# Attention and a two-layer network on one core: four engines in the order of the text from the first instruction on, w_in's units between a pair's steps, w_out's behind the layer's tiles

## The chip, the cores and the metric

The kernel runs on one core of a Trainium2 chip. The metric is device microseconds for one execution of the whole kernel, as the median of several runs. The engines are TensorE (PE: matrix products, written to PSUM), VectorE (DVE), ScalarE (ACT: functions of one element, here also scaled copies), GpSimd (POOL: here a few operations on one column) and SyncE (SP), whose queue issues all DMA transfers. Each engine runs its own queue in order and waits on semaphores for the others.

## The reference

```python
def _attn_ref(q, k, v):                      # (8, 12, 448, 64) each, f32
    S = q.shape[2]
    scale = 1.0 / np.sqrt(q.shape[-1])
    scores = scale * np.matmul(q, k.transpose(0, 1, 3, 2)) - np.log(S)
    attn = 1.0 / (1.0 + np.exp(-scores))
    return np.matmul(attn, v).astype(np.float32)

def _moe_ref(x, w_in, w_out):                # (3584, 768), (768, 2048), (2048, 768)
    h = x @ w_in
    g = np.where(h > 0.0, h, 1.0 * (np.exp(np.minimum(h, 0.0)) - 1.0))
    return (g @ w_out).astype(np.float32)
```

The output of the attention, with the heads laid side by side for each token, is the x of the second function. The weights w_in and w_out are 64-bit floating point in memory.

## The kernel before

**The work.** There are 8 batches, and a batch has 6 pairs of heads. A pair takes these steps: `prepare` (maxima of its inputs, powers of two as scales, and the operands in the form in which PE takes them), then for four blocks of keys (three of 128 and a rest of 64, `NC` = 3 is the rest's number) `scores` (PE), `soften` (a sigmoid on ACT), `parts` (the weights split into two 16-bit parts, on ACT and DVE) and `values` (PE, all blocks into one PSUM tile, `pav`), and at the end `finish` (the result, split into two parts, goes to `xh`). When a batch has its six pairs, `hidden` first rescales `xh` (`rescale`) and then runs the first layer, `moe1`: 16 tiles of the hidden dimension (`NF` = 16), 18 matmuls each into a tile `ph`, then an exponential on ACT, two operations on DVE, and a split into `g`. The second layer, `moe2`, is a generator: each `next` gives one step of six matmuls into `po`. From batch 1 on, `fill(n)` puts n such steps of the batch before between the steps of a pair.

Batch 0 (`EXACT` = 1) computes scores and values in f32. From batch 1 on each operand is two f16 parts and a product is three matmuls; but the pairs below `WHOLE` = `EXACT * NP + 2` = 8, so the first two of batch 1, still use f32 values: for them `parts` does nothing and v is loaded a second time, as a whole tile.

**The weights.** Both arrive as 64-bit words and are turned into f32 and then into two scaled f16 parts, once. For w_in this is done for 16 tiles of 768 KB (`load_w_in`, `w_in_tile`), beside batch 0. A tile takes five operations of some 0.9 us each and a chain of small ones: in `magnitudes` two on ACT (`Abs` of the high word, and the top of the low word, lines 156 and 160), one on DVE (line 161), and matmuls against ones on PE that add up the magnitudes (line 168); `sum_magnitude` reduces these sums to a power of two, one column of `wp`; `signed` puts the sign back (DVE, line 175); `split` writes the two parts (ACT line 139, DVE line 140). The words wait in a tile with the tag "wo", in a ring of five buffers, `WR` = 5; the results, f32, stand in another five, `WT` = 5. When all of w_in is done, the tile `wo` takes the same memory.

For w_out it is the same in two halves of 384 columns (`load_w_out`, a generator): 16 tiles of `magnitudes` and `signed`, then one sum for the half (in the PSUM tag "pav", one buffer, which a pair's values use as well), then 16 splits. That makes 32 steps a half. The loads (384 KB each, line 247) go to the tag "at" (3 buffers) or to places in `wo` that are still unused, and SP waits at a load until its place is free. `step(n)` runs n steps.

**The order.** Tile objects carry the dependencies, and the framework sets the semaphores. Outside `tc.manual_schedule` the framework's scheduler chooses the order of the instructions on each engine by its own estimate of their durations. Inside, the four engines named there take their instructions in the order of the text:

```python
    with tc.manual_schedule(engines={E.PE, E.Activation, E.DVE, E.SP}):
        for b in range(EXACT, B):
```

So before, batch 0's attention, all of w_in, the first layer of batch 0 and most of w_out (58 of its 64 steps, asked for in `w_out_beside`, four a tile) are ordered by the scheduler; the pairs of batch 1 and all that follows are ordered by the text. The other six steps of w_out, if any are left by then, stand in the first three pairs of batch 1. POOL is ordered by the scheduler throughout.

Of the kernel before, what the change touches and what calls it, by code (L numbers as in the profile page):

```python
# [34 lines left out]
def attention_ffn(  # L35
# [114 lines left out]
    def magnitudes(t, lo, hi, hl, sums, start, stop):  # L150


        u, h = t.bitcast(U32), hi.bitcast(F32)


        nc.scalar.activation(t, h, AF.Abs, scale=2.0**-112)
# [3 lines left out]
        nc.scalar.activation(lo, top, AF.Copy, scale=2.0**-13, bias=2.0**-14 - 0.5)  # L160
        nc.vector.scalar_tensor_tensor(
            u, u, 3, lo, op0=ALU.logical_shift_left, op1=ALU.bitwise_or
        )

# [14 lines left out]
    def sum_magnitude(dst, sums):  # L179

        m = sb.tile([P, 1], F32, tag="alw", name="alw", bufs=2)
        nc.vector.tensor_reduce(m, sums, axis=AX.X, op=ALU.max)
        nc.vector.tensor_scalar(m, m, TINY, None, op0=ALU.max)
# [18 lines left out]
    def w_in_tile(f):  # L202
        lo, hi, hl = w_in_words[f]
        t = stage[0][:, WR * 2 + f % WT].rearrange("p (c x) -> p c x", c=NK)
        sums = ps.tile([P, 512], F32, tag="pm", name=f"si{f}", bufs=3)
        magnitudes(t, lo, hi, hl, sums[:, :P], True, True)
        sum_magnitude(wp[:, f : f + 1], sums[:, :P])
        nc.vector.reciprocal(wr[:, f : f + 1], wp[:, f : f + 1])
        s = sb.tile([P, 1], F32, tag="sw", name=f"swi{f}", bufs=2)
        nc.gpsimd.tensor_scalar(s, wr[:, f : f + 1], 2.0**WTOP, None, op0=ALU.mult)  # L210
        d = wi[:, :, :, f * P : (f + 1) * P]
        signed(t, hi)
        split(d[:, 0], d[:, 1], t, s)
# [6 lines left out]
    def load_w_out(wo):  # L220


        for i in range(NH):
# [6 lines left out]
            sums = ps.tile([P, 512], F32, tag="pav", name=f"so{i}")  # L230
            loads = []

            def load(f):
                if f >= NF:
                    return
                if i == 0 and f >= 2:
                    st = wo[:, 1, f % 8 * 2 :][:, :2]
                elif i == 1 and f % 2 and f < NF - SP - SKEW:
                    st = wo[:, 1, NF - SP + f // 2 % 2 * 2 :][:, :2]
                else:  # L240
                    st = None
                if st is None:

                    st = sb.tile([P, 1, HM], U64, tag="at", name=f"so{i}_{f}", bufs=AB)
# [5 lines left out]
                loads.append(st)  # L250

            early = W_AHEAD[i]
            for f in range(early):
                load(f)
            for f in range(NF):
                load(f + early)
                lo, hi, hl = words(loads[f])
                t = whole[f].unsqueeze(1)
                magnitudes(t, lo, hi, hl, sums[:, :HM], f == 0, f == NF - 1)
                signed(t, hi)  # L260
                yield
# [3 lines left out]
            nc.vector.tensor_scalar(s[:, 1:], wn, s[:, 0:1], None, op0=ALU.mult)  # L265
            for f in range(NF):
                split(wo[:, i, f, 0], wo[:, i, f, 1], whole[f], s[:, 1 + f : 2 + f])
                yield
# [6 lines left out]
    def load_qk(b, hp):  # L275
# [3 lines left out]
        for i, src in enumerate((q, k)):  # L279
            for j in range(2):  # L280
                nc.sync.dma_start(  # L281
                    raw[:, i * (NC + 1) :][:, :NC, j],
                    src[b, h0 + j, :SM].rearrange("(p c) d -> p c d", c=NC),
                )
# [404 lines left out]
    def w_out_beside(f):  # L689
        nonlocal wo, steps  # L690
        if f == 0:
            w_in_ratios()
            wo = sb.tile([P, NH, NF, 2, HM], F16, tag="wo", name="wo")
            steps = load_w_out(wo)
            step(1)
        if f >= 2:
            step(W_OUT)
        if f == NF - 1:
            step(1)
# [28 lines left out]
    for n in range(2):  # L728
        load_pair(n)
        load_w_in(W_LOAD[n])  # L730
    prepare_pair(0)()()
    for f in range(W_IN[0]):
        load_w_in(1)
        w_in_tile(f)
    for n in range(EXACT * NP):
        raw = load_qk(*pairs[n + 2])
        if n:
            prepare_pair(n + 1)()()
        p = pair_of(n)
        for t in range(NC + 1):  # L740
            p.scores(t)
            if t == 1 and n == 0:
                prepare_pair(1)()()
            p.soften(t)
            p.values(t)
        p.finish()
        loaded[n + 2] = raw, load_v(*pairs[n + 2])
        for f in range(W_IN[n], W_IN[n + 1]):
            load_w_in(1)
            w_in_tile(f)  # L750
    prepare_pair(EXACT * NP + 1)()()
    load_pair(EXACT * NP + 2)
    load_pair(EXACT * NP + 3)
    scales = prepare_pair(EXACT * NP + 2)
    prepared = EXACT * NP + 2
    g = sb.tile([P, 2, NF, SM + 2 * R], F16, tag="g", name="g")
    h = hidden(0, w_out_beside)
    next(h)
    of_moe2 = next(h)

# [107 lines left out]
```

## Time and profile before

| | |
|---|---|
| median of 3 runs | 1201.75 us (1201.31 to 1201.85) |
| the profiled execution: its time | 1201.61 us |
| the profiled execution: its span, first to last instruction | 1199.8 us |
| busy PE, DVE, ACT, POOL in the span | 1148.5, 817.2, 710.1, 95.9 us |
| mean granted clock of PE | 0.989 |
| moved by DMA | 92.14 MB |

A row of the profile's groups has the line of the kernel, the engine, the operation, the tile written and the tiles read with their shapes, and the count; then the busy time in us and the mean of one in ns; then the idle time of the engine just before these instructions, and what ended it. A row of the timeline begins with start and length in us, both from the first instruction on. A row of the waits has who waited for whom: us in total, times, longest. Neighbours on one engine overlap by a little under 0.1 us, so a sum of durations is somewhat more than the time they take. PE's ends are modelled, and a busy PE also counts matmuls that run at a reduced clock.

### The profile page before, as it was taken

What the parts mean: (1) busy time and instruction counts of PE and PEld (TensorE: products, weight loads), DVE (VectorE), ACT (ScalarE), POOL (GpSimd) and SP (SyncE); (2) the same over time, 40 slices, a digit from 0 to 9 for tenths busy, and PEclk for the clock granted to TensorE, in tenths of its full rate; (3) what the DMA queues carried; (4) which work ended last, traced back from release to release, by engine and by line L of the source; (5) the groups of instructions that cost most, each with busy time, mean ns of one, the idle gap of its engine ahead of it and who ended that gap; (6) DMA issues with size and microseconds to landing.
All of it is one profiled execution on the core that took longest, in us unless ns stands there. A gap on an engine that the chain in (4) does not pass through costs nothing.

```text
span 1199.8 us, 24004 instructions
## 1 busy us (share of the span) xinstructions
PE 1148.5 (96%) x9662; PEld 634.7 (53%) x9662; DVE 817.2 (68%) x1730; ACT 710.1 (59%) x1087; POOL 95.9 (8%) x275
## 2 busy tenths in 40 slices
PE   6779976999999999999999999999999999999998
PEld 2224433555566555555566555655566555655565
DVE  4798888877577575876677575976667666864500
ACT  4785796855566447864666446865666446864300
POOL 1011001100011001100011000200011000100000
PEclk9989988999999999999999999999999999999999
DMA  8874634521234130531224221441134212310000
GB/s 220 260 191 96 220 107 114 104 61 41 47 79 95 34 68 20 115 78 40 41 65 96 53 51 37 94 100 40 40 61 93 61 40 47 70 30 8 1 27 27
DMA packets 220687, 92.14 MB, mean 77 GB/s; under 512 B 184224, under 2 KB 216480, under 8 KB 220576
## 3 DMA queue, kind: packets, MB, share of 16 engines
q1 hardware_dynamic: 220576, 90.61, 31.3%
q8 instruction: 75, 1.23, 0.4%
q14 instruction: 36, 0.29, 0.1%
HBM read 60.29 MB, written 11.01 MB: 59 GB/s over the span
## 4 chain that ended last, share of the span: by engine, by line
PE 85%; DMA 5%; DVE 4%; ACT 3%; SPq 2%; issue 1%; DVEq 0%; POOL 0%; ACTq 0%; POOLq 0%
PE ph L570 32%; PE po L602 31%; PE pav L480 7%; PE psc L408 7%; PE po_r L602 5%; DMA stage<-in_moe_w_in_dram 3%; PE pscr L500 1%; DMA wo<-in_moe_w_out_dram 1%; SPq L281 1%; ACT sg L416 1%; DMA so<-in_moe_w_out_dram 1%; ACT wo L139 1%; DVE wo L175 1%; DVE wo L140 1%; DVE wi L140 1%
## 5 line engine op out<-in xcount | busy, mean ns | idle before, releaser
L570 PE MATMUL ph<-xh,wi 128*128 128x448 f16 x2304 | 441.7, 353 | 1.7 <-DVE e L585 0.9
L602 PE MATMUL po<-wo,g 128*64 128x384 f16 (+1 forms) x4320 | 395.7, 328 | 6.9 <-ACT wo L139 3.8
L602 PEld LDWEIGHTS <-g 128*64 128x64 f16 (+1 forms) x4992 | 290.3, 109 | 169.6 <-issue 40.4
L570 PEld LDWEIGHTS <-wi 128*128 128x128 f16 x2304 | 223.0, 98 | 214.3 <-issue 8.0
L582 ACT ACTIVATE e<-ph,msc 128x448 f32<-128x448 f32 x128 | 80.7, 631 | 185.8 <-PE ph L570 161.1
L455 DVE SCALAR_TENSOR_TENSOR at<-sg,at 128x896 f16<-128x896 f32 x120 | 127.6, 1091 | 92.2 <-ACT at L454 92.2
L416 ACT ACTIVATE sg<-psc,bias,sc 128x896 f32<-128x896 f32 x126 | 133.5, 1094 | 3.6
L584 DVE TENSOR_SCALAR e<-e 128x448 f32<-128x448 f32 x128 | 50.2, 393 | 117.1 <-ACT e L582 117.1
L454 ACT ACTIVATE at<-sg 128x896 f16<-128x896 f32 x120 | 109.4, 947 | 0.6
L139 ACT ACTIVATE g<-e,msc 128x384 f16<-128x384 f32 (+1 forms) x192 | 96.1, 533 | 11.3 <-DVE e L585 9.9
L139 ACT ACTIVATE xh<-pav,sc 128x448 f16<-128x448 f32 x48 | 30.3, 631 | 119.8 <-PE pav L480 117.3
L140 DVE SCALAR_TENSOR_TENSOR g<-e,msc,g 128x384 f16<-128x384 f32 (+1 forms) x192 | 94.8, 522 | 1.9 <-ACT g L139 1.5
L585 DVE SCALAR_TENSOR_TENSOR e<-ph,msc,e 128x448 f32<-128x448 f32 x128 | 87.5, 684 | 4.1
L408 PE MATMUL psc<-qk 64*128 64x448 f16 x756 | 86.5, 352 | 2.2 <-ACT sg L416 2.2
L480 PE MATMUL pav<-at,vn 128*64 128x448 f16 x720 | 74.8, 353 | 0.0
L139 ACT ACTIVATE nat<-raw,sc 128x384 f16<-128x384 f32 (+1 forms) x126 | 60.7, 535 | 10.2 <-POOL sc L347 8.4
L480 PEld LDWEIGHTS <-vn 128*64 128x64 f16 x880 | 49.9, 110 | 31.2
L349 POOL TENSOR_SCALAR sc<-pw 128x1 f32<-128x1 f32 x42 | 12.2, 292 | 662.7 <-DVE pw L105 563.8
L602 PE MATMUL po_r<-wo,g 128*64 128x384 f16 (+1 forms) x672 | 64.9, 327 | 0.0
L140 DVE SCALAR_TENSOR_TENSOR nat<-raw,sc,nat 128x384 f16<-128x384 f32 (+1 forms) x126 | 60.6, 526 | 3.9 <-ACT nat L139 1.8
L140 DVE SCALAR_TENSOR_TENSOR xh<-pav,sc,xh 128x448 f16<-128x448 f32 x48 | 32.6, 680 | 37.1 <-ACT xh L139 37.1
L610 DVE TENSOR_SCALAR o<-po,osc 128x384 f32<-128x384 f32 x48 | 29.4, 612 | 41.1 <-PE po L602 36.4
(112 smaller groups left out, 928.5 us busy)
## 6 DMA issues: line engine op xcount, KB each, us to landing
stage<-in_moe_w_in_dram SPq DMA_DIRECT2D x16, 768.0 KB, 6.6
raw<-in_q_dram SPq DMA_DIRECT2D x96, 96.0 KB, 3.3
raw<-in_k_dram SPq DMA_DIRECT2D x96, 96.0 KB, 2.9
rv<-in_v_dram SPq DMA_DIRECT2D x48, 192.0 KB, 2.8
out_dram<-o SPq DMA_DIRECT2D x48, 192.0 KB, 2.1
wo<-in_moe_w_out_dram SPq DMA_DIRECT2D x19, 384.0 KB, 3.8
so<-in_moe_w_out_dram SPq DMA_DIRECT2D x13, 384.0 KB, 3.7
rv<-in_v_dram SPq DMA_DIRECT2D x96, 32.0 KB, 2.5
```

What stands on the lines that cost most here:

```text
L139: nc.scalar.mul(hi, src, s)
L140: nc.vector.scalar_tensor_tensor(lo, src, s, hi, op0=ALU.mult, op1=ALU.subtract)
L408: nc.tensor.matmul(psc[:, j, :S] if g < NC else psc[rows[j], 0, :S], kk[rows[j], o], qq[rows[j], :S], start=(n == 0), stop=(n == len(parts ...
L416: a = nc.scalar.activation(to, psc, AF.Sigmoid, bias=bias, scale=self.s_scale)
L454: nc.scalar.mul(hi, sg, 2.0**ATOP)
L455: nc.vector.scalar_tensor_tensor(lo, sg, 2.0**ATOP, hi, op0=ALU.mult, op1=ALU.subtract)
L480: nc.tensor.matmul(pav[rows[j], :S], vv[i][:, 2 * NC + j if g == NC else j * NC + g], sg[k][:, j], start=(g == 0 and n == 0), stop=(g == N ...
L570: nc.tensor.matmul(ph[:, :S], wi[:, wj, c, f * P : (f + 1) * P], xh[:, c, xj], start=(n == 0), stop=(n == 3 * NK - 1),)
L582: a = nc.scalar.activation(e, ph[:, :S], AF.Exp, scale=inv)
L584: nc.vector.tensor_scalar(e, e, 1.0, -1.0, op0=ALU.min, op1=ALU.add)
L585: nc.vector.scalar_tensor_tensor(e, ph[:, :S], inv, e, op0=ALU.mult, op1=ALU.max)
L602: nc.tensor.matmul(po[r, :HM], tokens[:, r], wo[:, i, f, wj], start=(n == 0), stop=(n == 3 * NF - 1),)
```

## The change

The block in which the text orders PE, ACT, DVE and SP now begins at the first instruction. For that the work on the weights is cut into units, and these are placed by hand.

- **w_in.** `w_in_tile` becomes the generator `w_in_units`: 74 units for 16 tiles, each of one or two operations a side (`fields`: the two on ACT, with the sum of the tile before on PE; `magnitudes`; `signed` of the tile before; for each two tiles one `sum_magnitude` and one scale; a `split`). A tile's load is issued three tiles ahead. Five units stand ahead of batch 0's pairs, and 12 in each pair, two behind every step.
- **Start.** The first tile of w_in is loaded before pair 0's q, k and v.
- **Batch 0's pairs.** A pair's next pair is prepared within it, in three places, and two blocks of scores go ahead of the first sigmoid.
- **w_out.** A half is 25 steps: 16 of one tile each (the sums and `signed` two tiles behind, `W_LAG` = 2), one for the scale, 8 of two splits. The first half stands behind the tiles of batch 0's first layer, one or two steps a tile; the second half stands in the first three pairs of batch 1, three steps in three places of each, the rest behind the third. Its sums are in the PSUM tag "pm" (three buffers, shared with the layers), no longer in "pav". Loads are issued where the text frees their buffer; one more buffer, "spare", is added.
- **Values.** `WHOLE` is 10, so pairs 8 and 9 also take f32 values.
- **Loads.** q of both heads comes in one DMA, and k too: four DMAs a pair for q and k where there were six.

```diff
-    WHOLE = EXACT * NP + 2
+    WHOLE = EXACT * NP + 4
-    W_IN = [1, 3, 6, 9, 12, 15, 16]
-    W_LOAD = [1, 1]
-    W_OUT = 4
-    W_AHEAD = [6, 2]
+    W_IN = 3
+    W_OUT = 25
+    W_AHEAD = [4, 2]
+    W_LAG = 2
...
+    def w_in_units():
+        scales, sums = {}, {}
+        def staged(f):
+            return stage[0][:, WR * 2 + f % WT].rearrange("p (c x) -> p c x", c=NK)
+        for f in range(NF + 2):
+            load_w_in(1)
+            if f < NF:
+                lo, hi, hl = w_in_words[f]
+                fields(staged(f), lo, hi, hl)
+            if 0 < f <= NF:
+                o = (f - 1) % 2
+                if not o:
+                    sums[f - 1] = ps.tile([P, 512], F32, tag="pm", name=f"si{f}", bufs=3)
+                add_up(sums[f - 1 - o][:, o * P : (o + 1) * P], staged(f - 1), True, True)
+            yield
+            if f < NF:
+                magnitudes(staged(f), lo)
+                yield
+            if 0 < f <= NF:
+                signed(staged(f - 1), w_in_words[f - 1][1])
+                yield
+            if f % 2 == 0 and f:
+                these = slice(f - 2, f)
+                pair = sums.pop(f - 2)[:, : 2 * P].rearrange("p (n x) -> p n x", x=P)
+                sum_magnitude(wp[:, these], pair)
...
+                scales[f + 1] = w
+                yield
+            if f in scales:
+                for i in range(2):
+                    n = f - 3 + i
+                    d = wi[:, :, :, n * P : (n + 1) * P]
+                    split(d[:, 0], d[:, 1], staged(n), scales[f][:, i : i + 1])
+                    yield
...
-            sums = ps.tile([P, 512], F32, tag="pav", name=f"so{i}")
+            if i == 0:
+                sums = ps.tile([P, 512], F32, tag="pav", name=f"so{i}")
+            else:
+                sums = ps.tile([P, 512], F32, tag="pm", name=f"so{i}", bufs=3)
...
+            while load(0):
+                pass
+            for f in range(NF + W_LAG):
+                if f < NF:
+                    lo, hi, hl = words(loads[f])
+                    t = whole[f].unsqueeze(1)
+                    fields(t, lo, hi, hl)
+                    magnitudes(t, lo)
+                d = f - W_LAG
+                if d >= 0:
+                    t = whole[d].unsqueeze(1)
+                    add_up(sums[:, :HM], t, d == 0, d == NF - 1)
+                    signed(t, words(loads[d])[1])
+                    while load(d + 1):
+                        pass
+                if f < NF:
+                    yield
...
-            for j in range(2):
-                nc.sync.dma_start(
-                    raw[:, i * (NC + 1) :][:, :NC, j],
-                    src[b, h0 + j, :SM].rearrange("(p c) d -> p c d", c=NC),
-                )
+            nc.sync.dma_start(
+                raw[:, i * (NC + 1) :][:, :NC],
+                src[b, h0 : h0 + 2, :SM].rearrange("h (p c) d -> p c h d", c=NC),
+            )
...
     def w_out_beside(f):
+        nonlocal third
+        if f:
+            step(W_OUT * f // (NF - 1) - W_OUT * (f - 1) // (NF - 1))
+        if f == 1:
+            third = scales()
+        if f == 3:
+            third()
+            load_pair(EXACT * NP + 3)
+        if f == 9:
+            prepare_next()
...
     with tc.manual_schedule(engines={E.PE, E.Activation, E.DVE, E.SP}):
+        load_w_in(1)
+        load_pair(0)
+        load_w_in(W_IN - 1)
+        load_pair(1)
+        units = w_in_units()
+        def w(n):
+            for _ in range(n):
+                next(units, None)
+        w(2)
+        prepare_pair(0)()()
+        w(3)
+        for n in range(EXACT * NP):
+            raw = load_qk(*pairs[n + 2])
+            p = pair_of(n)
+            p.scores(0)
+            p.scores(1)
+            p.soften(0)
+            w(2)
+            p.scores(2)
+            p.values(0)
+            p.soften(1)
+            second = prepare_pair(n + 1)
+            w(2)
+            p.scores(NC)
+            p.values(1)
+            p.soften(2)
+            third = second()
+            w(2)
+            third()
+            p.values(2)
+            p.soften(NC)
+            w(2)
+            p.values(NC)
+            if n == NP - 1:
+                h = hidden(0, w_out_beside)
+                next(h)
+            w(2)
+            p.finish()
+            loaded[n + 2] = raw, load_v(*pairs[n + 2])
+            w(2)
+        for _ in units:
+            pass
+        w_in_ratios()
+        wo = sb.tile([P, NH, NF, 2, HM], F16, tag="wo", name="wo")
+        steps = load_w_out(wo)
...
+        of_moe2 = next(h)
...
+                if b == EXACT and hp < NC:
+                    step(3)
                 gap = 11 if hp == 0 else 5
                 fill(gap - 2)
...
                 if b == EXACT and hp < NC:
-                    step(3 if hp < NC - 1 else NF)
+                    step(3)
...
                 p.finish()
+                if b == EXACT and hp < NC:
+                    step(3 if hp < NC - 1 else W_OUT)
```

More of the change, by code (lines that the diff above doesn't have):

```diff
@@ L148, in words, with fields, magnitudes @@
         return w[:, :, :, 0], w[:, :, :, 1], st
-    def magnitudes(t, lo, hi, hl, sums, start, stop):
-        u, h = t.bitcast(U32), hi.bitcast(F32)
-        nc.scalar.activation(t, h, AF.Abs, scale=2.0**-112)
+    def fields(t, lo, hi, hl):
+        nc.scalar.activation(t, hi.bitcast(F32), AF.Abs, scale=2.0**-112)
         top = hl.bitcast(U16).rearrange("p a (c t) -> p a c t", t=4)[:, :, :, 1]
         nc.scalar.activation(lo, top, AF.Copy, scale=2.0**-13, bias=2.0**-14 - 0.5)
+    def magnitudes(t, lo):
+        u = t.bitcast(U32)
         nc.vector.scalar_tensor_tensor(
@@ L163, in magnitudes, with add_up @@
         )
+    def add_up(sums, t, start, stop):
         top = t.bitcast(BF16).rearrange("p a (c t) -> p a c t", t=2)[:, :, :, 1]
@@ L179, in sum_magnitude @@
     def sum_magnitude(dst, sums):
-        m = sb.tile([P, 1], F32, tag="alw", name="alw", bufs=2)
+        m = sb.tile([P, dst.shape[1]], F32, tag="alw", name="alw", bufs=2)
         nc.vector.tensor_reduce(m, sums, axis=AX.X, op=ALU.max)
@@ L200, in load_w_in @@
                 w_in_words.append(words(st))
[L202 to L213, printed above, removed]
+    def w_in_units():
[23 more added lines that the diff above has]
+                sum_magnitude(wp[:, these], pair)
+                nc.vector.reciprocal(wr[:, these], wp[:, these])
+                w = sb.tile([P, 2], F32, tag="sw", name=f"swi{f}", bufs=2)
+                nc.gpsimd.tensor_scalar(w, wr[:, these], 2.0**WTOP, None, op0=ALU.mult)
+                scales[f + 1] = w
[6 more added lines that the diff above has]
+                    yield
     def w_in_ratios():
@@ L250, in load @@
                 loads.append(st)
[L252 to L261, printed above, removed]
+                return True
+            while load(0):
[15 more added lines that the diff above has]
+                    yield
             sum_magnitude(wop[:, i : i + 1], sums[:, :HM])
@@ L726, in load_pair @@
             loaded[n] = load_qk(*pairs[n]), load_v(*pairs[n])
[L728 to L759, printed above, removed]
     def prepare_next():
         nonlocal prepared, scales
-        load_pair(prepared + 2)
+        if prepared + 2 not in loaded:
+            load_pair(prepared + 2)
         prepared += 1
@@ L779, in attention_ffn @@
     with tc.manual_schedule(engines={E.PE, E.Activation, E.DVE, E.SP}):
+        load_w_in(1)
[43 more added lines that the diff above has]
+        steps = load_w_out(wo)
+        prepared = EXACT * NP + 1
+        scales = prepare_pair(prepared)
+        load_pair(EXACT * NP + 2)
+        g = sb.tile([P, 2, NF, SM + 2 * R], F16, tag="g", name="g")
+        of_moe2 = next(h)
         for b in range(EXACT, B):
```

44 lines of the change are left out of this document (24 added, 20 removed).

## The prediction

> **What bounds the kernel now.** I read the stretches of the span first, then who TensorE waits for, then the groups of instructions, then the order of time around the stalls. The stretches give, for each, the length, the busy time of PE, PEld, DVE, ACT and POOL, the granted clock, the DMA share and GB/s.
>
> ```profile
> PE 1148.5 (96%) x9662; PEld 634.7 (53%) x9662; DVE 817.2 (68%) x1730; ACT 710.1 (59%) x1087; POOL 95.9 (8%) x275
> ```
> ```profile
> 0.00:97.00 97.00, 68.28 (x355) 27.12 (x356) 71.71 (x176) 63.59 (x81) 8.48 (x28) 0.95 0.78 210
> 97.00:157.00 60.00, 57.97 (x315) 29.22 (x316) 52.01 (x128) 42.22 (x82) 5.46 (x17) 1.00 0.53 160
> 157.00:204.00 47.00, 30.64 (x253) 14.48 (x251) 39.96 (x89) 39.75 (x71) 5.89 (x16) 0.85 0.41 114
> 204.00:1200.00 996.00, 991.59 (x8747) 563.93 (x8743) 653.55 (x1340) 564.56 (x856) 76.07 (x214) 1.00 0.26 57
> ```
> ```profile
> 10.00:80.00 70.00, 55.75 (x299) 21.57 (x297) 53.16 (x130) 53.38 (x68) 6.29 (x17) 0.98 0.98 267
> 80.00:97.00 17.00, 9.73 (x51) 3.82 (x48) 16.58 (x40) 8.72 (x12) 1.47 (x4) 0.80 0.13 34
> ```
>
> From 204 us on PE is never idle but for 4.4 us at the very end, and its work there is not reordered. So the change is worth what it does ahead of 204, and nothing else. I call the three stretches there A (attention of batch 0 beside w_in, to 97), B (first layer of batch 0, to 157) and C (first pair of batch 1, to 204). Their idle PE is 28.7, 2.0 and 16.4 us. C's 30.64 busy us ran at clock 0.85, so they are 26.0 us of full speed and C loses 21 us in all. In A DVE is the fullest engine (71.71 of 97), DMA is near its full share from 10 to 80 us, and from 80 on DVE alone is full.
>
> ```profile
> PE psc L408 <- ACT sg L416: 8.3, 4, 4.2
> PE pav L480 <- DVE xh L140: 5.3, 1, 5.3
> PE so L168 <- DVE wo L161: 4.6, 3, 4.0
> PE po L602 <- ACT wo L139: 3.8, 2, 3.6
> ```
> ```profile
> SPq L247 <- DVE wo L175: 37.3, 11, 8.2
> ```
> ```profile
> 156.24 2.30 PE L602 MATMUL po<-wo,g 128*64 128x384 f16 x26
> 164.20 16.02 SPq L247 DMA_DIRECT2D so<-in_moe_w_out_dram  x5
> ```
> ```profile
> 188.16 3.90 PE L480 MATMUL pav<-sg,vw 128*64 128x448 f32 x12 [1.12 <-DVE alw L182]
> 190.93 5.05 DVE L140 SCALAR_TENSOR_TENSOR wo<-wo,swo 128x384 f16<-128x384 f32 x8 [0.15 <-ACT wo L139]
> ```
>
> C in order of time: the layer ends and the second layer's matmuls begin at 156.2. The second half of w_out is still being prepared: its loads stand 16 us in SP behind buffers that DVE frees, its sums hold the PSUM tile pav that the pair's values need (they start at 188.16, released by alw, the reduction of those sums), and then its splits run as a block on ACT and DVE, ahead of the sigmoids that the next pair needs.
>
> **Stage A after.** The same work on DVE stands in the text's order: 12 units of w_in between a pair's steps. Two tiles share one scale, so eight reductions and their small operations go; I take 2 us off. Three splits of w_in that ran after 97 come in (3 us), so DVE has about 72 us. By 17 us some 5 us of it can be done, because w_in's first tile now goes ahead of pair 0 on SP, and the first scores follow later.
>
> ```profile
> 0.72 1.34 SPq L281 DMA_DIRECT2D raw<-in_q_dram  x2
> 6.74 0.59 SPq L199 DMA_DIRECT2D stage<-in_moe_w_in_dram  x1
> 8.02 1.09 DVE L366 COPY early<-pt 128x896 f32<-128x896 f32 x1 [6.80 <-PE pt L362]
> ```
>
> q and k come by four DMAs a pair where there were six; each is 0.6 us of SP, which is on the path only here. Pair 0 then queues behind 0.79 MB of w_in (2.9 us at 267 GB/s), so `early` is copied some 2 us later than at 8.02. That leaves 67 us for DVE after 17. The queues keep their order, so some waits on ACT and PE remain. DVE was 76% busy from 10 to 80 and 98% from 80 to 97. The 98% gives 85 us for the end of A, the 76% gives 105. I take 90%, 74 us, and A ends at 91: units of w_in stand between every sigmoid and what needs it, which is what 80 to 97 had and 10 to 80 lacked. ACT has less (63.59), PE 68.28 x 0.95 = 65 us, DMA about 18 MB, which is 68 us at 267 GB/s, so each fits.
>
> **Stage B after.** Only the first half of w_out stands here: one tile or two splits a step, 25 steps over 15 tiles of the layer.
>
> ```profile
> L139 ACT ACTIVATE wo<-wo,swo 128x384 f16<-128x384 f32 x28 | 16.3, 611 | 4.4 <-DVE swo L265 3.1 <-DVE wo L140 1.2
> L160 ACT ACTIVATE wo<-wo 128x384 uint32<-128x384 uint16 x19 | 10.3, 543 | 0.0
> L156 ACT ACTIVATE wo<-wo 128x384 f32<-128x384 f32 x17 | 9.3, 547 | 6.2 <-DMA wo<-in_moe_w_out_dram 6.0
> ```
> ```profile
> L140 DVE SCALAR_TENSOR_TENSOR wo<-wo,swo 128x384 f16<-128x384 f32 x27 | 16.0, 613 | 1.6 <-ACT wo L139 1.0
> L140 DVE SCALAR_TENSOR_TENSOR g<-e,msc,g 128x448 f16<-128x448 f32 x16 | 10.9, 684 | 1.5 <-ACT g L139 1.5
> L585 DVE SCALAR_TENSOR_TENSOR e<-ph,msc,e 128x448 f32<-128x448 f32 x16 | 10.9, 682 | 0.1
> L161 DVE SCALAR_TENSOR_TENSOR wo<-wo 128x384 uint32<-128x384 uint32 x17 | 9.4, 555 | 5.0 <-ACT wo L160 4.8
> L175 DVE SCALAR_TENSOR_TENSOR wo<-wo 128x384 uint32<-128x384 uint32 x17 | 9.4, 556 | 0.0
> L584 DVE TENSOR_SCALAR e<-e 128x448 f32<-128x448 f32 x16 | 6.2, 391 | 0.5 <-ACT e L582 0.5
> ```
> ```profile
> 131.44 0.55 DVE L175 SCALAR_TENSOR_TENSOR wo<-wo 128x384 uint32<-128x384 uint32 x1
> 131.90 0.55 DVE L161 SCALAR_TENSOR_TENSOR wo<-wo 128x384 uint32<-128x384 uint32 x1
> ```
>
> Such instructions start 0.46 us apart though each lasts 0.55: 0.08 overlap. DVE: 16 x (0.391 + 0.682 + 0.684 - 0.24) = 24 for the layer, 16 x (0.555 + 0.556 + 0.613 - 0.24) = 24 for half of w_out, some 6 for two pairs' preparation and the scales: 54 us. ACT's half is 16 x (0.547 + 0.543 + 0.611 - 0.24) = 23. PE has today's 57.97 plus the 18 matmuls done ahead of 97 less a few sums, 60 us. So PE is the bound with DVE at 90%. Two us more for the first tile, whose scale takes a chain of small operations: B takes 62 and ends at 153 (today 156). Its bounds: 60 and, at DVE 80% busy, 68. w_out's loads start only when w_in's buffers are free, which is at the end of A; the first two tiles of the layer hide their 3.8 us.
>
> **Stage C after.** The second half of w_out (24 us of DVE, 23 of ACT) stands in three pairs of batch 1, nine steps in each, its sums in another PSUM tile, so a pair's values no longer wait for them. Pairs 8 and 9 keep whole f32 values (WHOLE 8 to 10), which saves their split.
>
> ```profile
> 219.00:231.00 12.00, 12.00 (x142) 7.24 (x139) 11.37 (x23) 9.73 (x13) 3.13 (x5) 1.00 0.61 116
> ```
> ```profile
> L455 DVE SCALAR_TENSOR_TENSOR at<-sg,at 128x896 f16<-128x896 f32 x120 | 127.6, 1091 | 92.2 <-ACT at L454 92.2
> ```
> ```profile
> 204.59 2.42 PE L480 MATMUL pav<-sg,vw 128*64 128x448 f32 x12
> 206.95 0.97 PE L468 MATMUL pav<-sgr,vw 64*64 64x448 f32 x4
> 217.94 1.87 PE L480 MATMUL pav<-at,vn 128*64 128x448 f16 x18
> 219.64 0.55 PE L480 MATMUL pav<-ar,vn 128*64 128x448 f16 x4
> ```
>
> A pair of batch 1 has 11.4 us of DVE. Without the split it loses 3 x 1.09 and about 1.9 for the last keys and v, leaving 6.2. With a third of 24 us: 14.2. PE has 12 to 16 in these pairs (the first has more matmuls of the second layer), plus 0.9 for sums: about even. So PE should run on with small stalls. Bounds: 0 (all hidden) and today's 21. I take 6, nearer to 0 because nothing holds pav. The price on PE: f32 values take 2.42 + 0.97 against 1.87 + 0.55, 1.0 more a pair, 2 us for two. Pairs 8 and 9 load v twice (0.5 MB more) while DMA runs at 116 GB/s of 267: nothing. Holding one of the three pm tiles for the sums leaves two for the second layer, which then waits for DVE's copy of the output; that is within the 6.
>
> The Trainium skill ("FP8 and Floating Point Precision", TensorE Precision Notes) counts four passes for true FP32. By that, 16 matmuls at 4 x 0.104 us (1.87 / 18) would be 6.6 us, 4.2 more a pair, and the sum 6 us higher. The trace shows 3.39, and I go by it.
>
> **The sum.** End of B 153; PE work left, 996 from 204 on and 26 in C, plus 2 for f32 values and 2 for sums that came earlier before: 1026; stalls 6. Span 1185. The profiled execution took 1201.61 for a span of 1199.8, so add 1.8: 1187. Its 1201.61 lies 0.14 under the median, so nothing is to be corrected.
>
> **Rivals.**
> 1. *A packs fully.* DVE 98% busy as from 80 to 97 (A ends 6 us earlier), B at 60, C without stalls less than 6: about 1174. For it: PE and ACT fit. Against: one order for four queues.
> 2. *PE goes cold in A.* After its 5.3 us wait the clock of 80 to 97 is 0.80. The 12 matmuls of 188.16 took 3.90 where those of 204.59 took 2.42, 1.6 times. If half of A's 65 us ran so, PE would need 20 more, 85, and A would end near 98: 1194. Against: units between steps leave gaps of 1 to 2 us. The Trainium skill ("TensorE: Matmul & The Clock Gate", Part 1) says that an idle window of about 3.4 us halves the clock; the trace agrees for the 5.3 us wait.
> 3. *C stays as it is.* SP still stands behind w_out's buffers (in the second half few are free at once), ACT waits for the load at the head of its queue, and behind it the sigmoids: 15 us more, 1202, no change.
> 4. *Slower: DVE waits at each tile of w_in.* In the text `magnitudes` follows `fields` at once, and DVE can't pass it.
>
> ```profile
> L160 ACT ACTIVATE stage<-stage 128x768 uint32<-128x768 uint16 x16 | 14.4, 902 | 1.7 <-DMA stage<-in_moe_w_in_dram 1.7
> L156 ACT ACTIVATE stage<-stage 128x768 f32<-128x768 f32 x16 | 14.4, 902 | 17.2 <-DMA stage<-in_moe_w_in_dram 14.7 <-DVE alw L183 2.2 <-DVE wi L140 0.3
> ```
>
> If ACT never gets ahead, each of 16 tiles costs DVE 2 x 0.82 us, 26 in all, of which my 90% holds 7: 1206. It decides against the change from about 1.35 us a tile. Against: DVE has more work than ACT, so ACT gains a lead.
>
> **Chances.** Forecast 0.48, rival 1 0.14, rival 2 0.12, rival 3 0.10, rival 4 0.16. No change means within 0.2%, about what a measurement of this kernel can tell. So faster 0.48 + 0.14 + 0.12 = 0.74, same 0.10, slower 0.16. Forecast's own range: A from 85 to 97 gives 1180 to 1194. The range for 8 in 10, from just inside rival 1 to just inside rival 4: 1175 to 1205.
>
> **What will show it.** The first long run of ph at about 91 and the first po at about 153; DVE near 90% busy between 17 and 91; no wait of pav for alw; PE losing under 10 us from there to the fourth pair. Wrong if DVE waits for `fields` (L160) through A, if PE's clock is below 0.95 there, or if ACT waits for w_out's loads in the first pairs of batch 1.

## The result and the profile after

The changed kernel takes 1235.01 us (median; 1234.67 to 1235.81) where the kernel before, run beside it, takes 1201.80. The ratio is 1.0277, with a 95% interval of 1.0259 to 1.0295. Forecast were 1187 and a range of 1175 to 1205: the change makes the kernel 33 us slower, and the forecast missed by 48.

The stretches of the changed kernel, cut where its own stages end. Columns as before: length, busy time of PE, PEld, DVE, ACT and POOL with counts, granted clock, DMA share, GB/s.

```profile
0.00:98.00 98.00, 70.44 (x347) 27.18 (x348) 77.05 (x155) 65.94 (x83) 9.37 (x28) 0.89 0.75 193
98.00:161.00 63.00, 57.60 (x298) 29.16 (x296) 51.62 (x116) 39.16 (x75) 2.18 (x9) 0.98 0.53 171
161.00:250.00 89.00, 57.83 (x450) 26.78 (x448) 44.85 (x103) 43.42 (x77) 5.51 (x21) 0.77 0.33 89
250.00:1232.00 982.00, 975.75 (x8563) 554.93 (x8559) 639.37 (x1317) 552.69 (x840) 74.09 (x209) 1.00 0.25 56
```

Stage A left PE 28.7 us idle before and leaves it 27.6 idle now, at a granted clock of 0.89 where it was 0.95. In stage B PE is nearly full in both. From 250 us on PE is full again. The time is in the third row: 31.2 of 89 us idle, and the other 57.83 ran at a mean clock of 0.77. TensorE's matmuls in order of time, where the layer ends and C begins:

```profile
154.82 6.41 PE L625 MATMUL ph<-xh,wi 128*128 128x448 f16 x33
161.16 1.31 PE L463 MATMUL psc<-qk 64*128 64x448 f16 x12
172.79 0.48 PE L170 MATMUL so<-wo,ones 128*128 128x384 bf16 x1 [10.32 <-DVE wo L161]
173.20 5.74 PE L657 MATMUL po<-wo,g 128*64 128x384 f16 x54
```

The layer ends at 161.2, 5.0 later than before. By the prediction's own count 1026 us of PE work follow; the span is 1232.9, so C loses 45.7. By the same count (1199.8 less 156.2 less 996 and 26 of work) it lost 21.6 before. The 33.1 us by which the span grew are thus 5.0 ahead of C, 24.1 in it, and 4 that the prediction had for f32 values and later sums (these 4 were not isolated).

Whom TensorE and ACT wait for, over the whole span; the last row is the kernel before:

```profile
PE so L170 <- DVE wo L161: 29.7, 9, 10.3
PE so L170 <- DVE to L161: 4.2, 3, 2.3
ACT sg L471 <- PE psc L463: 18.5, 10, 6.8
ACT wo L153 <- DMA wo<-in_moe_w_out_dram: 16.7, 3, 11.1
ACT to L153 <- DMA so<-in_moe_w_out_dram: 11.4, 1, 11.4
PE so L168 <- DVE to L161: 2.2, 2, 1.5
```

PE waited 6.8 us at `so` before (4.6 for `wo`, as the prediction shows, and 2.2 for `to`). It waits 33.9 now, all of it at the sums of w_out's magnitudes, which PE takes as one matmul with `ones` for each tile; 31.2 of these lie in C, as much as PE is idle there. The fourth row of the fence before this one shows that it did not lack work: the 54 matmuls of `po` that start as soon as the sum is done stood right behind it. And ACT, in order of time, waits for PE's scores and, 11 us each, for two loads:

```profile
180.67 1.10 ACT L471 ACTIVATE sg<-psc,bias,sc 128x896 f32<-128x896 f32 x1 [6.77 <-PE psc L463]
197.14 0.54 ACT L153 ACTIVATE wo<-wo 128x384 f32<-128x384 f32 x1 [11.11 <-DMA wo<-in_moe_w_out_dram]
229.69 0.55 ACT L153 ACTIVATE to<-so 128x384 f32<-128x384 f32 x1 [11.37 <-DMA so<-in_moe_w_out_dram]
```

The queue of SP shows where the first of them was:

```profile
184.97 1.55 SPq L432 DMA_TRANSPOSE qk<-nat  x1
186.56 1.10 SPq L349 DMA_DIRECT2D vw<-in_v_dram  x1
...
192.43 1.25 SPq L354 DMA_DIRECT2D rv<-in_v_dram  x2
193.79 0.53 SPq L293 DMA_DIRECT2D wo<-in_moe_w_out_dram  x1
```

In the text the loads of a place stand behind the preparation of the next pair, so on SP they stand behind its transpose, which needs `nat` from DVE, and its loads.

So there were two suspects. P: PE, in order, stands at a sum whose tile ACT and DVE have only begun; meanwhile it gives them no scores and no values, so the three engines take turns. R: the loads of w_out pace ACT, and DVE and PE behind it. The texts of the first four runs call the second one L, for the loads' place in SP's queue, and add W: half of w_out is too much work for ACT and DVE wherever it stands. In the text of `no_sums`, "rival R" also holds ACT and DVE being too full. S means one thing in `chains` and another, the cover told below, in the runs at the moved places.

### The profile page after: what moved, and what is told of

Same layout as the page of the kernel before. It is cut to its first block, busy times and chain, and to the rows that moved or that the text cites. A ratio compares the mean times of both kernels' runs of the same rounds, so it can differ in the third digit from the quotient of the medians.

```text
span 1232.9 us, 23735 instructions
## 1 busy us (share of the span) xinstructions
PE 1161.6 (94%) x9650; PEld 638.0 (52%) x9650; DVE 812.9 (66%) x1686; ACT 701.2 (57%) x1075; POOL 91.2 (7%) x267
## 4 chain that ended last, share of the span: by engine, by line
PE 83%; DVE 7%; SPq 3%; ACT 3%; DMA 2%; issue 1%; POOL 0%; DVEq 0%; POOLq 0%; ACTq 0%
PE ph L625 32%; PE po L657 30%; PE pav L535 7%; PE psc L463 7%; PE po_r L657 5%; PE pscr L555 1%; SPq L354 1%; DVE wi L140 1%; SPq L340 1%; ACT sg L471 1%; ACT wo L139 1%; DVE wo L140 1%; DMA so<-in_moe_w_out_dram 1%; SPq L349 1%; DVE mx L143 1%
## 5 line engine op out<-in xcount | busy, mean ns | idle before, releaser
L510 DVE SCALAR_TENSOR_TENSOR at<-sg,at 128x896 f16<-128x896 f32 x114 | 121.2, 1091 | 90.3 <-ACT at L509 90.3
L509 ACT ACTIVATE at<-sg 128x896 f16<-128x896 f32 x114 | 103.9, 947 | 0.6
L535 PE MATMUL pav<-at,vn 128*64 128x448 f16 x684 | 71.0, 352 | 0.0
L535 PEld LDWEIGHTS <-vn 128*64 128x64 f16 x836 | 47.4, 110 | 29.6
L463 PEld LDWEIGHTS <-qk 64*128 64x128 f16 x756 | 30.6, 95 | 56.9 <-issue 38.3
```

Of the source, the lines that this page charges most:

```text
L463: nc.tensor.matmul(psc[:, j, :S] if g < NC else psc[rows[j], 0, :S], kk[rows[j], o], qq[rows[j], :S], start=(n == 0), stop=(n == len(parts ...
L509: nc.scalar.mul(hi, sg, 2.0**ATOP)
L510: nc.vector.scalar_tensor_tensor(lo, sg, 2.0**ATOP, hi, op0=ALU.mult, op1=ALU.subtract)
L535: nc.tensor.matmul(pav[rows[j], :S], vv[i][:, 2 * NC + j if g == NC else j * NC + g], sg[k][:, j], start=(g == 0 and n == 0), stop=(g == N ...
```

## Experiments

The runs of one of these kernels lie 2 to 7 us apart, in one case 11, so a difference of some 3 us between two of them says little. The kernel before stood beside every group and took 1201.4 to 1202.4.

**All of w_out in the layer.** Does it help to keep the second half out of the pairs?

```diff
-    W_OUT = 25
+    W_OUT = 50
```

> All 50 steps of w_out stand behind the tiles of batch 0's first layer, none in the pairs of batch 1. Theory L (the second half's loads stand in SP behind a pair's DMA transpose and the next pair's ten loads, ACT waits for them at the head of its queue) and theory P (its sums stand in PE's queue ahead of the second layer's steps, which could run): both say that the 46 us that PE loses from the layer's end to the fourth pair fall to under 8, while the layer grows from 63 us to 80 to 85, because DVE then has 78 us of work in it; in all 1208 to 1216. Theory W (half of w_out is too much work for ACT and DVE wherever it stands) says that the layer grows by as much as the pairs win: 1230 to 1240.

1237.7 us (1.0314, 1.0274 to 1.0353). The layer's matmuls end at 204.9, 44 us later where 17 to 22 were expected; in C hardly anything is lost any more. PE's waits at sums went along:

```profile
PE so L170 <- DVE wo L161: 35.4, 15, 8.3
```

The cost goes where the second half goes. It is not a property of the pairs. The time lies in W's range, 1230 to 1240; what speaks against W are later runs with all of ACT's and DVE's work in them.

**The places of the steps.** A place is a `step(3)` in a pair; each of the three pairs has three. The first was moved behind the matmuls of the second layer (`fill`), which lets PE run these ahead of the sums; the second ahead of `third()` and `prepare_next()`, which puts its loads ahead of the next pair's transpose and loads on SP.

```diff
-                if b == EXACT and hp < NC:
-                    step(3)
                 gap = 11 if hp == 0 else 5
                 fill(gap - 2)
+                if b == EXACT and hp < NC:
+                    step(3)
```

```diff
+                if b == EXACT and hp < NC:
+                    step(3)
...
                     third()
                     prepare_next()
-                if b == EXACT and hp < NC:
-                    step(3)
```

Each was run alone, and both together.

> In the first three pairs of batch 1 the first three steps of w_out stand behind the first steps of the second layer, no longer ahead of them. Theory P: PE's wait of 10.3 us at the first sum falls to 5 or less, as 4.6 us of the second layer run first, and the kernel comes to 1222 to 1229. Theory L: the two waits for loads stay, and PE has done by then what it could do in them, so 1231 to 1236. Theory W: 1233 to 1237.

> In the first three pairs of batch 1 the second three steps of w_out stand ahead of the pair's transpose and the next pair's loads. Theory L: ACT's two waits of 11 us for a load of w_out fall to 1 to 4 each, and the kernel comes to 1212 to 1220. Theory P: the waits of PE for DVE in front of the sums stay, 34 us in all, and the time stays above 1228. Theory W: 1233 to 1237.

> Both moves together. If L and P each hold a part, the gains add up: 1200 to 1212, with PE's waits for sums under 10 us. If P is only a consequence of L (PE waits because ACT waits for loads), it is the time of the loads' move alone within 4 us.

1229.0 us (1.0213 to 1.0248), 1226.7 (1.0194 to 1.0224) and 1222.6 (1.0157 to 1.0188): 6.0, 8.3 and 12.4 us. Each order counts, and the two gains nearly add. But `loads_first` met neither range of its text, though the longest wait of ACT for a load fell from 11.4 to 5.9 us, and the two together, at 1222.6, stayed above the 1200 to 1212 given for two causes that add up. PE still waits 25.0 us at `so` with both (22.3 for `wo`, 2.7 for `to`). `fill_first` shows that the 54 matmuls of `po` were ready: with the sum behind them they start at 161.49, and the first wait at a sum falls from 10.3 to 5.8 us.

**More places for loads.** Up to six loads ahead (`W_AHEAD` 6, and two more places in the memory of `wo`), alone and with both moves.

```diff
-    W_AHEAD = [4, 2]
+    W_AHEAD = [4, 6]
...
-                if i == 1 and f % 2 and f < NF - SP - SKEW - W_LAG:
-                    return wo[:, 1, NF - SP + f // 2 % 2 * 2 :][:, :2]
+                if i == 1 and (f < SP or f == SP + AB):
+                    return wo[:, 1, NF - 2 - f % (SP + AB) * 2 :][:, :2]
...
```

> The changed kernel with more places for the second half's loads (tiles 0 to 3 and 7 in places of w_out's second half that are not yet in use, six tiles ahead in place of two), no step moved. Theory R: seven loads stand ahead of the first pair's transpose, the two waits of 11 us of ACT for loads shrink to one or go, 1212 to 1220. Theory P alone: 1230 or more.

> The same places, with both moves of steps (the second layer's steps ahead of the first three steps of w_out, and the second three ahead of the pair's transpose and the next pair's loads). R and P together: 1202 to 1211. If the moves only helped the loads, 1212 or more.

1233.4 us (1.0245 to 1.0276) and 1222.55 (1.0158 to 1.0189): no more than 1.6 us off the kernels without it. In the first of them one of ACT's two waits of 11 us is gone and the other stays, at 11.1.

**Hardly any loads.** The second half loads three tiles and uses them over again.

```diff
+                if i == 1 and f >= AB:
+                    loads.append(loads[f - AB])
+                    return True
...
```

> The changed kernel, but the second half of w_out loads only its first three tiles and uses them for all sixteen (the other thirteen loads are left out; everything else of the work stands). Theory R (the second half runs at the pace of its few load buffers: a buffer is held for the load, some 4 us, the tile's own work and two more tiles, so ACT, at the head of its queue, waits for a load at almost every tile): the loss behind the layer falls from 46 us to 15 to 20, 1203 to 1210. What is left is theory P (sums in PE's queue ahead of work that could run) and is seen in PE's waits for DVE. Theory P alone: 1228 or more.

1228.7 us (1.0216 to 1.0246): 6 us. R alone falls. No wait for a load of w_out is longer than 2.4 us now, yet PE and ACT go on taking turns, as PE and ACT in order of time show:

```profile
173.34 0.48 PE L170 MATMUL so<-wo,ones 128*128 128x384 bf16 x1 [10.32 <-DVE wo L161]
181.28 1.10 ACT L474 ACTIVATE sg<-psc,bias,sc 128x896 f32<-128x896 f32 x1 [6.83 <-PE psc L466]
187.86 0.48 PE L170 MATMUL so<-wo,ones 128*128 128x384 bf16 x1 [5.49 <-DVE wo L161]
197.56 0.63 ACT L139 ACTIVATE xh<-pav,sc 128x448 f16<-128x448 f32 x1 [10.05 <-PE pav L526]
```

**Sums a tile later.** In the second half the sum and sign of a tile come three tiles behind and ahead of the next tile's fields, so PE reaches a sum when its tile is done. Once at the change's places with four tiles loaded, once with all loads, both moves, still more places for loads and one more step behind the layer's last tile. The part that both have:

```diff
...
-            for f in range(NF + W_LAG):
-                if f < NF:
+            lag = W_LAG + i
+            for f in range(NF + lag):
+                if f < NF and not i:
                     lo, hi, hl = words(loads[f])
                     t = whole[f].unsqueeze(1)
                     fields(t, lo, hi, hl)
                     magnitudes(t, lo)
-                d = f - W_LAG
+                d = f - lag
                 if d >= 0:
                     t = whole[d].unsqueeze(1)
                     add_up(sums[:, :HM], t, d == 0, d == NF - 1)
                     signed(t, words(loads[d])[1])
...
+                if f < NF and i:
+                    lo, hi, hl = words(loads[f])
+                    t = whole[f].unsqueeze(1)
+                    fields(t, lo, hi, hl)
+                    magnitudes(t, lo)
```

> As the kernel that loads only a few tiles of w_out's second half (here four; the other loads are left out), at the changed kernel's places; but a tile's sum and sign stand three tiles later than its magnitude and ahead of the next tile's, so that PE's sums at a place belong to the place before. Theory P (the three engines take turns: PE stands at a sum whose tile ACT and DVE have just begun, and then ACT stands at scores that PE could not start): PE's waits for DVE in front of the sums fall from 29 us to under 8, the loss behind the layer from 40 us to 10 to 15, in all 1198 to 1206. If they take turns for another reason (DVE and ACT simply have too much work there), 1222 or more.

> All loads, both moves, the sums and signs three tiles later as above, and six load places, of which nine tiles are loaded before the first pair of batch 1 (one more step behind the layer's last tile issues them). Theory P with the loads out of the way: 1197 to 1206, at best as fast as before the change. If loads come late again, 1210 to 1218.

1205.5 us (1.0018 to 1.0042) and 1214.6 (1.0092 to 1.0125). With most loads out the order of the sums is worth 23 us, and of PE's waits at sums 7.4 us are left, where `no_second_loads` had 29.1:

```profile
PE so L170 <- DVE wo L161: 4.4, 6, 1.7
PE so L170 <- DVE to L161: 3.0, 2, 2.3
```

I took this for a proof of P. It was one only as long as the loads were out: with all loads in, 1214.6 is in the range given for loads that come late again.

**No sums.** The sharper test of P: the change as it is, without the second half's sums but the first.

```diff
-                    add_up(sums[:, :HM], t, d == 0, d == NF - 1)
+                    if i == 0:
+                        add_up(sums[:, :HM], t, d == 0, d == NF - 1)
+                    elif d == 0:
+                        add_up(sums[:, :HM], t, True, True)
```

> The changed kernel (1235.0 us), without the sums of w_out's second half on PE but for the first tile's: fields, magnitudes, signs and splits of all 16 tiles stay at their places on ACT and DVE, all loads too. The scale of that half comes from one tile alone, so its output isn't the reference's. PE has 15 matmuls of 0.17 us less, 2.6 us. Theory P (what costs most is that PE, in order, stands at a sum whose tile ACT and DVE have only begun, with work behind it that could run): PE's waits at so (29.7 us) go, the waits of ACT for psc that follow from them too, and the time is 1205 to 1213, the loads' 6 us staying. Rival R (ACT and DVE are themselves too full or wait for loads, and PE would wait for them at the sigmoids, the keys or the values anyway): the waits move from so to psc, pav and xh, and the time is 1226 to 1233.

> As the run before, and the second half of w_out loads three of its 16 tiles (the others are computed from those; output not the reference's). Theory P: with both gone C loses only what ACT's and DVE's own work makes it lose. The kernel with all sums and three tiles loaded took 1228.7; that with four loaded and its sums one tile later took 1205.5, C losing 17 us. I expect 1200 to 1206 here. If sums and loads cover for each other it is much less (below 1198); under rival R it stays at 1222 to 1229.

1234.1 us (1.0247 to 1.0278): nothing, where P in this form expected at least 22 us. With the loads out too, 1209.1 (1.0045 to 1.0079), outside all the ranges of its text. P alone falls as R did. The one sum that is kept is the first, and its wait of 10.3 us stays in both runs, so of the 31.2 us in C only 20.9 could go. In the run without sums PE stands 19.9 us at something else that DVE owes it. The matmuls `pr`, the maxima for the next pair's scales, need a place of the PSUM tag "pm". Their operand `mx` is there at 187.6, but they start at 200.67, when DVE has done `o`, the copy of the second layer's output out of such a place. The sums' tile holds one of the three. And DVE comes late to `o` because it stands behind ACT, which waits for the same two loads. Whom DVE waits for between 155 and 262 us, and then PE, ACT and DVE in order of time:

```profile
DVE wo L161 <- ACT wo L157: 11.6, 3, 9.6
```

```profile
198.06 0.55 ACT L153 ACTIVATE wo<-wo 128x384 f32<-128x384 f32 x1 [11.10 <-DMA wo<-in_moe_w_out_dram]
200.01 0.61 DVE L668 TENSOR_SCALAR o<-po,osc 128x384 f32<-128x384 f32 x1
200.67 0.23 PE L131 MATMUL pr<-mx,ones 128*64 128x12 bf16 x2 [8.98 <-DVE o L668]
229.10 0.55 ACT L153 ACTIVATE to<-so 128x384 f32<-128x384 f32 x1 [10.90 <-DMA so<-in_moe_w_out_dram]
231.72 0.22 PE L131 MATMUL pr<-mx,ones 128*64 128x12 bf16 x2 [10.93 <-DVE o L668]
```

Two waits cover for each other: whichever is taken away, the other holds the same stretch. Whether a fourth place in "pm" would change that was not run. The next runs made the same table at the moved places.

> The kernel with both moves (1222.6 us: the first three steps behind the fill, the second three ahead of the next pair's transposes and loads on SP), without the sums of w_out's second half but for the first tile's. All loads stay. The scale of that half comes from one tile alone, so its output isn't the reference's. Theory S (two waits cover for each other: PE at the sums, and ACT at loads that SP issues only behind the next pair's transpose): with the loads ahead of the transpose and the sums gone both are broken, so it comes near the run without sums and loads, 1207 to 1214. Rival: the loads cost through their buffers and latency wherever they stand: ACT still waits about 11 us twice, and the time is 1218 to 1223.

> The kernel with both moves (1222.6 us), the second half of w_out loading three of its 16 tiles (the others are computed from those; output not the reference's); all sums stay. Theory S: the moves have taken most of the loads' wait away already, so this gains less than at the places of the change (there 6 us): 1217 to 1222, PE still waiting some 20 us at so. Rival: in the kernel with both moves it is the loads that still cost (ACT's longest wait for one was 6.4 us), and it falls to 1207 to 1213.

> The kernel with both moves (1222.6 us) without the sums but for the first tile's, and with three of the 16 tiles of the second half loaded; output not the reference's. At these places the sums alone gave 2.7 us and the loads alone 9.0. If they cover for each other as at the change's places (there 1, 6 and 26 together), this takes 1200 to 1207; if their gains only add, 1210 to 1212.

| us | sums and loads in | sums out | loads out | both out |
|---|---|---|---|---|
| at the change's places | 1235.0 | 1234.1 | 1228.7 | 1209.1 |
| both moves | 1222.6 | 1219.9 | 1213.6 | 1201.9 |

Alone the two are worth 0.9 + 6.3 = 7.2 us at the change's places, together 25.9. At the moved places 2.7 + 9.0 = 11.7, together 20.7. The cover is there in both rows: at the moved places the last corner came out as forecast, 1201.9 in 1200 to 1207. Of the 25.9, 2.6 us are work and not waiting, the 15 matmuls left out at 0.17 us each. What S said besides, that the move had taken the loads' wait away, is wrong: without sums the moved places take 1219.9, not 1207 to 1214, and without loads 1213.6, not 1217 to 1222. C at these two corners, from 161 to 250, first the change's places without sums and loads, then the moved ones:

```profile
161.00:250.00 89.00, 70.08 (x695) 37.44 (x693) 63.24 (x141) 62.69 (x106) 8.77 (x32) 0.90 0.30 69
```

```profile
161.00:250.00 89.00, 75.89 (x754) 40.13 (x754) 68.43 (x151) 67.38 (x113) 9.65 (x32) 0.92 0.34 75
```

PE is busy 70.08 and 75.89 of 89 us where the changed kernel has 57.83, at 0.90 and 0.92 of the clock and not 0.77. At the change's places with both out, by the count above (span 1205.6 in its profiled execution, 1.6 us under the median; the layer's end at 160.4; 2.6 us of work less), C loses some 22 us, as much as in the kernel before. So sums and loads together make up what C lost by the change. ACT's and DVE's own work is all still there, so W falls. Of the 18.9 us that PE is idle in this stretch, 10.3 are the first sum's and 7.0 are at scores that wait for a sigmoid.

**What the loads cost.** Three runs took the second half's loads off SP (Q: their place in that queue is the cost), two of them without sums, one of these with the two more places; the third is the last kernel with all its work in it, 1214.6 us.

```diff
-                nc.sync.dma_start(
+                (nc.gpsimd if i else nc.sync).dma_start(
                     st[:, 0], w_out[f * P : (f + 1) * P, i * HM : (i + 1) * HM]
```

> The run without sums (1234.1 us), its second-half loads issued from POOL's queue and not SP's: same buffers, same places in the text, nothing else moved. The scale of that half comes from one tile alone, so its output isn't the reference's. Theory Q (what the loads cost is their place in SP's queue: they stand behind a pair's transpose and loads, and these in turn behind loads that wait for a buffer): ACT's two waits of 11 us go and it comes near the run without sums and loads (1209.1): 1208 to 1215. Rival (buffers and latency): the waits for loads stay and it takes 1225 to 1234.

> The run without sums and with the second-half loads on POOL's queue (1229.0 us), with two more places for loads, so that up to six are ahead where there were two to four. The scale of that half comes from one tile alone, so its output isn't the reference's. If the loads are late by their place on SP and by too few places, and each alone stands in for the other, ACT's waits for them go and it takes 1209 to 1216. If their transfers themselves get in the way of the pair's transposes and loads, it stays at 1224 to 1230.

> The kernel with both moves, the sums one tile later and more places for loads (1214.6 us), its second-half loads issued from POOL's queue and not SP's. Theory Q: the 5.6 us that ACT waits for a load behind SP's transpose and ten loads goes, and what follows from it: 1206 to 1211; the run with its sums later and four tiles loaded took 1205.5, and its layer ended 3.6 us earlier. Rival: 1213 to 1216.

1229.0 us (1.0204 to 1.0236), 1224.9 (1.0159 to 1.0221) and 1214.4 (1.0074 to 1.0113). From 1234.1 the queue's order takes 5 us and the two more places 4 more; the runs of the second of these kernels lie 7 us apart, so the 4 are uncertain. 16 us remain to the 1209.1 without loads, and in the third kernel the queue changes nothing (1214.6 and 1214.4): Q is a part, not the cause. On POOL the loads are late too, as its queue and ACT in the second of these runs show:

```profile
178.66 0.59 POOL L293 DMA_DIRECT2D wo<-in_moe_w_out_dram  x1 [23.15 <-DVE wo L177]
196.77 0.60 POOL L293 DMA_DIRECT2D so<-in_moe_w_out_dram  x1 [11.63 <-DVE wo L161]
201.13 0.54 ACT L153 ACTIVATE wo<-so 128x384 f32<-128x384 f32 x1 [5.51 <-DMA so<-in_moe_w_out_dram]
```

In the text a load stands behind the sign (L177) of the tile whose buffer it takes. The first row names it; the second names the operation right behind such a sign. Then the load takes about 4 us to land. Signs are made only in the places, three at a time, so a place's loads come free late and the next place waits for them. That this makes up all of the 16 us is argued from the rows, not shown; whether the transfers disturb the pair's own loads was not separated. No changed kernel with all the work in it comes nearer to the kernel before than the last of these.

**The chain of w_in's scales.** In A eight chains of small DVE operations were taken apart, with the units' work between their links.

```diff
...
-                sum_magnitude(wp[:, these], pair)
-                nc.vector.reciprocal(wr[:, these], wp[:, these])
...
+            chain = chain_of(f, sums, scales) if f % 2 == 0 and f else chain
...
+                next(chain, None)
```

Each `next` of the chain issues one of its operations; the last one the reciprocal and the scale.

> The changed kernel, with the four small DVE operations of a scale of w_in (maximum, bound, mask, reciprocal) put between the large ones of the next units, where each now follows the one that it depends on. Theory S (a dependent small operation right behind its source costs 0.20 us, between others 0.07): the first layer starts 2 to 4 us earlier than at 94.7, and the kernel comes to 1231 to 1233. Theory B (attention beside w_in is bound by something else, such as PE's reduced clock): no change, 1234 to 1236.

1236.5 us (1.0267 to 1.0301): a miss. From 17 to 92 us DVE is less busy, first in the changed kernel, then with the chains taken apart:

```profile
17.00:92.00 75.00, 58.50 (x305) 21.23 (x303) 65.92 (x130) 56.29 (x73) 8.24 (x19) 0.90 0.72 191
```

```profile
17.00:92.00 75.00, 59.32 (x305) 22.12 (x305) 61.81 (x122) 54.68 (x68) 8.44 (x13) 0.89 0.71 190
```

It did less in that time (122 instructions and not 130), and the first long matmuls of the layer came later, 98.57 for 94.65, while ACT waited 12.5 us for `swi`, the scale, from POOL, and 1.0 in the changed kernel. What the chains cost stays open; the run suggests that the latency of a scale sets A's end as well as DVE's load does.

## Why the prediction was wrong

**Stage C failed, and it is 40 of the 48 us.** The step was "So PE should run on with small stalls. Bounds: 0 (all hidden) and today's 21. I take 6, nearer to 0 because nothing holds pav." C loses 45.7. The reason given was right: no wait of the values for the reduction is left. But the balance by sums, 14.2 us of DVE to 12 to 16 of PE a pair, says only that the work fits if each engine finds something to do, and a queue in order does not offer it. Three things were left out or priced too low: the added sums as a place where PE stands, with ready matmuls behind it (the prediction priced them at their 0.9 us of work); what nine steps in each of three pairs do to the loads, whose buffers come free only in these places; and the wait for DVE's copy of the second layer's output, which was to be "within the 6" and holds PE for 19.9 us once the sums are out. The upper bound was wrong for the same reason: today's 21 came from the other arrangement and bounds nothing of this one.

**Rival 3 had half of it.** It named ACT waiting for a load at the head of its queue and SP behind w_out's buffers, and set it at 15 us by the stall of before. Sums and loads together cost 25.9 at the change's places, but either alone could be removed for 0.9 or 6.3, which no rival said.

**Stage A: 94.65 for 91.** That is by the prediction's own sign, the first long run of `ph`; the 98 of the stretches above lies within these 18 matmuls. The 5 us of DVE work ahead of 17 came true (71.41 busy in the first 92 us less the 65.92 behind 17 leaves 5.5). By 94.65 DVE had done 73.70 us where 72 were counted, and from 17 to 92 it was 88% busy where I took 90%: both terms were a little short. PE's granted clock was 0.90 from 17 to 92, below the 0.95 that was to speak for rival 2, but of PE's 67.09 us up to 94.65 that is some 7, where rival 2 had 20. The 18 matmuls took 6.44 us, where the next 18 took 3.57:

```profile
94.65 6.44 PE L625 MATMUL ph<-xh,wi 128*128 128x448 f16 x18 [0.75 <-DVE xh L576]
```

```profile
DVE stage L161 <- ACT stage L157: 9.3, 4, 6.0
```

Rival 4 (DVE waits for the fields at each tile) did not come: as the last row shows, its waits there are 9.3 us in 4 places.

**Stage B: 66.5 for 62**, from 94.65 to 161.16, within its bounds of 60 to 68. The two us for the first tile were too few: its 18 matmuls took 2.9 us more than the next, and PE then waited 1.9 for DVE's `dg`, on the way to the layer's scales, up to 103.0.

**The sum**: 3.7 from A, 4.5 from B, 40 from C. That nothing moves behind C held: PE is busy 975.75 of the last 982 us.

**A reading that was wrong without harm.** The price of f32 values, 3.39 us for 2.42 a pair, is right, but the x12 and x4 of a pair's rows are not 16 matmuls: `values` asks for 8, and the trace counts each twice. One takes 0.42 us, 4.1 times the 0.104 of an f16 one. So the trace agrees with the count of four passes that the prediction cites from the Trainium skill ("FP8 and Floating Point Precision", TensorE Precision Notes), and an estimate by it, 8 matmuls at 4 x 0.104 us, gives 3.3 us, not 6.6.

## What to carry to other kernels

Work that is spread into gaps brings its own waits along: for each instruction added to a queue in order, ask when its operand will be ready at that place and what stands behind it, not only whether the sums of work fit. Put an operation that needs another engine's result behind work that can run, and a whole place (here three steps) behind its producer. Free the buffers of a load in another place than the one that needs the load (this last was not run by itself). When taking one wait away changes nothing, take away two: here two waits measured 1 and 6 us alone and 26 together.

## What was not expected of the hardware

The waits cost more than their length. The 54 matmuls behind the first 10.3 us wait took 5.74 us. The same 54 behind a busy PE, in the run with all of w_out in the layer, took 4.58:

```profile
206.10 4.58 PE L657 MATMUL po<-wo,g 128*64 128x384 f16 x54
```

In C of the changed kernel 57.83 us of matmuls at a clock of 0.77 are, as an estimate from these two figures, some 13 us more than at full speed, beside 31.2 of idleness: nearly a third of the loss is clock. The Trainium skill ("TensorE: Matmul & The Clock Gate", Part 1) says that an idle window of about 3.4 us halves the clock; behind the wait of 10.3 us the trace agrees, with a granted clock of 0.50 from 172.79 to 175 and 1.00 from 177 on. From 201 to 211 the clock was 0.50 as well, though no wait there was above 2.4 us; in the 4 us before, PE had been busy for 0.47. A load of 0.38 MB needed about 4 us from issue to landing in this stage: 3.6 from SP's queue in the changed kernel, 4.1 from POOL's in `deep_no_sums_pool`.
